# Splitting w2 in five staggered parts, and two key products on GpSimd

## The chip, the cores and the metric

One Trainium2 chip, one of its cores. The metric is the device time of one launch in microseconds (us). The engines of the core are TensorE (PE: matmul; PEld: weight load), VectorE (DVE), ScalarE (ACT), GpSimd (POOL) and SyncE (SP, which here only issues DMAs). Each engine runs its own instructions in the order in which the program gives them; an instruction that waits for a semaphore holds up all that stand behind it on that engine.

## What is computed

Polynomial sketch attention, whose result is the input of four dense experts that are mixed by normalized weights:

```python
def phi(x):
    a = np.einsum('rd,bhsd->bhsr', S1, x)
    b = np.einsum('rd,bhsd->bhsr', S2, x)
    return np.einsum('bhsi,bhsj->bhsij', a, b).reshape(*x.shape[:-1], r * r)
q_p, k_p = (phi(q), phi(k))
kv = np.einsum('bhsf,bhsd->bhfd', k_p, v)
z = np.sum(k_p, axis=2)
num = np.einsum('bhsf,bhfd->bhsd', q_p, kv)
den = np.einsum('bhsf,bhf->bhs', q_p, z)[..., None] + 1e-06
...
x = np.ascontiguousarray(attn_out.transpose(0, 2, 1, 3)).reshape(B * S, H * D)
p = domain_probs / (domain_probs.sum(-1, keepdims=True) + 1e-09)
for e in range(E):
    h = np.maximum(x @ w1[e], 0.0)
    out += p[:, e:e + 1] * (h @ w2[e])
```

The sizes: 4 batches, 4 heads, 1088 positions, head size 32, sketch size r = 8; 4352 tokens of width 128, 4 experts, hidden size 1024. All is float32.

## The kernel before

**Products of three matmuls.** A full float32 matmul of 448 columns stands in the profile as two matmuls of 0.92 us together (L1256), one of the `float32r` kind as one of 0.37 us. Most of the experts' matmuls are therefore made of three `float32r` ones, for which weights and data are split into a rounded part and rests:

- Tokens: `token_parts(m)` makes `xa` (ScalarE, `split`), `xb` and `xd` (VectorE, `join`) of one chunk of tokens.
- w1: `weight_part` makes `wa` (ScalarE), `wb` and `wd` (VectorE) of half an expert's w1. The list `SPLITS` has the step behind which each of these stands.
- w2: `second_weight_parts(e)` is a generator that makes `vab`, `vb` and `vd` of six of the eight row blocks of an expert's w2 (768 columns, handled as 256 and 512). It first splits with scale 4096 (ScalarE) and takes the difference (`join` on VectorE: the low part), then splits again with scale 1 over the same place (ScalarE), then forms `vd` (VectorE). The list `W2_AT` gives, for experts 2, 3, 0 and 1 in this order, the half step at which each next part of the generator is issued.

`split` is line 900 and `join` line 903 of the profile, whatever they are applied to. `vab` of an expert has the tag of that expert's w1, so it stands in the memory that held w1: its first split must wait until `wa` and `wb` have been made of it. The second split writes over what the low part was computed from, so it waits for VectorE's `join`.

**Steps and half steps.** The tokens go in 11 chunks m (`CHUNKS`: 128, 448, 480, 480, six of 448, 128). A step i is one chunk, one expert and one pair of hidden blocks (16 steps for each chunk), and has two half steps j; half step number 2i + j. In a half step of the chunks 1 to 9, `first` issues on TensorE `xa` by `wa` (L1150) and `xb` by `wb` (L1151) into a PSUM tile h; on ScalarE a correction of that tile in place (L1152); then, by `third`, for the half step before, `xd` by `wd` on top of it (L1202), and on ScalarE the rounded relu of it (`ha`, L1206, or the whole `hid`, L1211). `lower` issues the rests `hb` (L1178) and, for each pair, `hd` (L1181) on VectorE. So L1202 of one half step waits for L1152 of the same tile, and whatever ScalarE has ahead of that L1152 can hold up TensorE.

Then `work()` runs, and issues what the lists give for this half step: first the parts of w2 (`at_half`, from `W2_AT`, counted from 0), and then the entries of `plan` (counted from 1, so that entry 48 of `plan` comes in the same half step as entry 47 of `W2_AT`). What stands in `to_part` (the parts of w1 by `SPLITS`, the tokens by step 16m - 4 and 16m - 3) comes behind both half steps of a step.

**Products with w2.** `behind` issues what is due on TensorE. In chunk 1, experts 0 and 1 are taken `whole` (L1256, float32, `second`); from expert 2 on six blocks go in three matmuls (`passed`, L1275), in an order and at due times given by `DEAL` (a name such as a0 is the part and the block, the number its due half step, counted from the first of that expert). Two PSUM tiles, o0 and o1, hold the sums; `gather` adds them on VectorE (`ev`, L1304 and L1307) and multiplies with the gate and sums up on GpSimd (L1314, L1316).

**Attention beside it.** The attention of the later batches runs in between, by `plan`. `key_pieces(b, ...)` lays out the keys of batch b by `KEYS_AT[b]`: three transposes of k (L413), three projections on TensorE (L457) that ScalarE copies (L460), three sums (`fs`, L467), and then the four `key_product`s (L473, 128 x 576 elements each, all on VectorE) that make the factors `kp`; `key_sums` needs them only at entry 79. `UNITS_AT` lays out queries: products (L800), and a visit (`unit_visit`, `unit_project`, L683 to L709) with small matmuls at entry 47.

What matters for the change, for batch 1:

```python
    W2_AT = (36, 37, 38, 39), (40, 41, 42, 43), (44, 45, 46, 46), (50, 51, 53, 54)
    ...
        1: ((36, 37, 38), (38, 39, 40), (39, 40, 41), (51, 54, 60, 66)),
```

Of the kernel before, what the change touches and what calls it, by code (L numbers as in the profile page):

```python
# [17 lines left out]
def _ap(t, p0: int, np_: int, off: int, free):  # L18

    p = list(t.ap)[0]  # L20
    return bass.AP(t.tensor, t.offset + p0 * p[0] + off, [[p[0], np_]] + [list(d) for d in free])
# [3 lines left out]
def kernel(  # L25
# [24 lines left out]
    nc = tc.nc  # L50
# [9 lines left out]
    NT = 9  # L60
# [30 lines left out]
    ]  # L91
    W2_AT = (36, 37, 38, 39), (40, 41, 42, 43), (44, 45, 46, 46), (50, 51, 53, 54)
    TOKENS_AT = 11, 12

    CHUNKS = [P, 448, 480, 480] + [448] * 6 + [P]
# [15 lines left out]
    def psum(pool, tag):  # L111
        return pool.tile([P, 512], F32, tag=tag, name=tag)
# [32 lines left out]
    def load_batch(b):  # L145
        load_rows(k, b, "kn")
        vn[b] = load_v(b)
# [129 lines left out]
    low = _ap(s_raw, 0, R2, 0, [[2, D]])  # L277
# [133 lines left out]
    def key_turn(b, r, t0=0, n=4):  # L411
        if r < 2:
            nc.vector.transpose(  # L413
                _ap(kT, 0, P, 512 * r + P * t0, [[P, n], [32, 4], [1, 32]]),
                _ap(kn[b], 0, P, P * r + 32 * t0, [[32, n], [8 * D, 4], [1, 32]]),
            )
        else:
            nc.vector.transpose(kT[:, 1024:S], kn[b][:, 1024:S])

    def value_copy(b):  # L420
        copy = nc.gpsimd.tensor_copy if b == 1 else nc.scalar.copy
        for r in range(2):
            copy(
                vx[:, 4 * r : 4 * r + 4, :, 0:D].rearrange("p t h d -> p h t d"),
                _ap(vn[b], 0, P, P * r, [[8 * D, H], [D, 4], [1, D]]),
            )
            yield
        copy(vx[0:64, 8, :, 0:D], _ap(vn[b], 0, 64, 1024, [[D, H], [1, D]]))
# [21 lines left out]
    def key_project_wide(b, gi, kf):  # L450

        t0, n = FG[gi]
        if gi == 0:
            fss[b] = apool.tile([P, 2, NT, 32], F32, tag="fs", name="fs")
            kps[b] = apool.tile([P, NT, 2, P], F32, tag="kp", name="kp")
        for t in range(n):
            nc.tensor.matmul(  # L457
                kf[:, P * t : P * t + P], kT[:, P * (t0 + t) : P * (t0 + t + 1)], sk[:, :], start=True, stop=True
            )
        nc.scalar.copy(  # L460
            _ap(fss[b], 0, P, 32 * t0, [[32 * NT, 2], [32, n], [1, 32]]), _ap(kf, 0, P, 0, [[32, 2], [P, n], [1, 32]])
        )

    def key_add(b, gi, kf):
        t0, n = FG[gi]
        fs = _ap(fss[b], 0, P, 32 * t0, [[32 * NT, 2], [32, n], [1, 32]])
        nc.vector.tensor_tensor(out=fs, in0=_ap(kf, 0, P, HP, [[32, 2], [P, n], [1, 32]]), in1=fs, op=ALU.add)  # L467

    def key_product(b, t0, n, p, x, eng, kf=None):

        if b:
            fs = lambda k, dims: _ap(fss[b], 0, P, 32 * (NT * p + t0) + R2 * x + k, [[32, n]] + dims)
            eng.tensor_tensor(  # L473
                out=_ap(kps[b], 0, P, 256 * t0 + P * p + R * x, [[256, n], [R2, R], [1, R]]),
                in0=fs(0, [[1, R], [0, R]]), in1=fs(R, [[0, R], [1, R]]), op=ALU.mult,
            )
            return
        src, off = (kf, P * p) if kf is not None else (fss[b], 32 * (NT * p + t0))
        eng.tensor_tensor(
            out=_ap(kps[b], 0, P, 256 * t0 + P * p + 64 * x, [[256, n], [32, 2], [R, 4], [1, R]]),  # L480
            in0=_ap(src, 0, P, off + 4 * x, [[32, n], [R2, 2], [1, 4], [0, R]]),
            in1=_ap(fss[b], 0, P, 32 * (NT * p + t0) + R, [[32, n], [R2, 2], [0, 4], [1, R]]),
            op=ALU.mult,
        )
# [35 lines left out]
    def key_pieces(b, turn, project, summed, products):  # L520

        for r in range(3):
            add(turn[r], lambda r=r: key_turn(b, r))
        values, kf = value_copy(b), {}

        def project_keys(gi):
            kf[gi] = psum(ps_h, "h")
            key_project_wide(b, gi, kf[gi])

        def sum_keys(gi):  # L530
            key_add(b, gi, kf[gi])
            next(values, None)
            if gi == 2 and 1 < b < B - 1:
                load_batch(b + 1)

        for gi in range(3):
            add(project[gi], lambda gi=gi: project_keys(gi))
            add(summed[gi], lambda gi=gi: sum_keys(gi))
        for i, (p, x) in enumerate(((0, 0), (0, 1), (1, 0), (1, 1))):
            add(products[i], lambda p=p, x=x: key_product(b, 0, NT, p, x, nc.vector))  # L540

    sums = {}

# [205 lines left out]
    turned, factors, products = {}, {}, {}  # L749
# [59 lines left out]
    def add(hs, run):  # L809

        plan.setdefault(hs, []).append(run)

    FIRST_AT = (1, 2, 4, 5, 7, 9, 10, 12, 14, 15, 15, 15, 17, 18, 18, 19, 21, 23, 23)
    KEYS_AT = {
# [3 lines left out]
    }  # L818
# [6 lines left out]
    def lay_plan():  # L825
# [31 lines left out]
        for b in range(1, B):  # L857
            key_pieces(b, *KEYS_AT[b])
            if b > 1:
                add(UNITS_AT[{2: 2, 3: 4}[b]][3], lambda b=b: key_end(b))  # L860
# [38 lines left out]
    def split(a, w, scale):  # L899
        nc.scalar.activation(a, w, ACTF.Copy, scale=scale * NEAR)  # L900

    def join(out, in0, scale, in1, op):
        nc.vector.scalar_tensor_tensor(out=out, in0=in0, scalar=scale, in1=in1, op0=ALU.mult, op1=op)  # L903

    def weight_part(what, e, h):

        c = slice(F // 2 * h, F // 2 * (h + 1))
        w, a, b, d = (x[:, c] for x in (w1_of[e], wa[:, e], wb[:, e], wd[:, e]))
        if what == "a":
            split(a, w, 4096.0)  # L910
        elif what == "b":
            join(b, w, -4096.0, a.bitcast(F32), ALU.add)
        else:
            join(d, a.bitcast(F32), -R12, b.bitcast(F32), ALU.subtract)
# [3 lines left out]
    def second_weight_parts(e):  # L918


        w, n = w2_of[e, 0], N3 * DM
        vab = cpool.tile([P, F], F32R, tag=f"w1_{e}", name="vab")
        vb = cpool.tile([P, 2 * n - F], F32R, tag=f"vb_{e}", name="vb")
        a, lows = vab[:, 0:n], [(0, F - n, vab[:, n:F]), (F - n, n, vb[:, :])]
        for c, z, b in lows:
            split(a[:, c:z], w[:, c:z], 4096.0)
            join(b, w[:, c:z], 4096.0, a[:, c:z].bitcast(F32), ALU.subtract)
            yield
        for c, z, b in lows:
            split(a[:, c:z], w[:, c:z], 1.0)  # L930
            if c == 0:
                yield
        d = cpool.tile([P, n], F32R, tag=f"w2_{e}0", name="vd")[:, :]
        for c, z, b in lows:
            join(d[:, c:z], b.bitcast(F32), 1.0, a[:, c:z].bitcast(F32), ALU.subtract)
        w2_parts[e] = {
            THREE[i]: tuple(
                x[:, DM * i - c : DM * i - c + DM] for x, c in ((a, 0), next((x, c) for c, z, x in lows if DM * i < z), (d, 0))
            )
            for i in range(N3)  # L940
        }
        yield
# [393 lines left out]
    def at_step(step, *calls):  # L1336
        to_part.setdefault(step, []).extend(calls)
# [4 lines left out]
    for what, e, h, step in SPLITS:  # L1342
        at_step(step, lambda p=(what, e, h): weight_part(*p))
    for e, at in zip((2, 3, 0, 1), W2_AT):
        parts_of = second_weight_parts(e)
        for hs in at:
            at_half.setdefault(hs, []).append(next_of(parts_of))
# [135 lines left out]
```

## Time and profile before

| | |
|---|---|
| median of 3 runs | 447.97 us (447.76 to 448.28) |
| the profiled execution, its own time | 448.23 us |
| its span in the profile | 446.5 us |
| TensorE busy | 440.3 us, 2988 matmuls |
| TensorE weight loads | 370.7 us |
| VectorE busy | 380.5 us, 627 instructions |
| ScalarE busy | 335.0 us, 715 instructions |
| GpSimd busy | 135.5 us, 219 instructions |
| granted TensorE clock | 1.00 |

How to read it: in the timeline a row has the start in us, the length in us, the engine, the line of the kernel, the operation, the tile written and the tiles read, the shapes and the number of instructions; in brackets the idle time of the engine just before, and what ended it. In the table of stretches a row has the stretch, its length, the busy time of each engine with the number of instructions, then the granted clock, the share of the DMA engines and GB/s. A row of the waits has who waited for whom, the sum in us, how often, and the longest. Lengths of neighbouring instructions overlap a little, since they are pipelined; the distance of two starts is what one costs its engine.

### The profile page before, as it was taken

How to read it: one execution, taken by the hardware profiler on the slowest of the kernel's cores; microseconds unless marked ns; L12 is line 12 of the kernel's file. 1: busy time of each engine (PE TensorE's matmuls, PEld its weight loads, DVE VectorE, ACT ScalarE, POOL GpSimd, SP SyncE). 2: the span in 40 equal slices, each digit the busy share in tenths (PEclk: the TensorE clock that was granted, in tenths of full speed). 3: DMA queues.
4: the chain of work that ended last, by engine and by line, in shares of the span. 5: the costliest groups of instructions: out<-in, count | busy, mean ns of one | idle time of the engine just before them, and what ended most of it. 6: DMA issues, size and time to landing. Idle time of an engine off the chain costs nothing.

```text
span 446.5 us, 8575 instructions
## 1 busy us (share of the span) xinstructions
PE 440.3 (99%) x2988; PEld 370.7 (83%) x2988; DVE 380.5 (85%) x627; ACT 335.0 (75%) x715; POOL 135.5 (30%) x219
## 2 busy tenths in 40 slices
PE   9999899999999999999999999999999999999997
PEld 6887568878887888888888888888888888888886
DVE  5997879988999889888987888899988898898853
ACT  4477888867877588868875888787888888888831
POOL 7348324210143123213321333133323413331430
PEclk9999999999999999999999999999999999999999
DMA  6966257323702250145014601351300020027401
GB/s 186 282 176 169 62 132 156 94 45 96 186 22 46 67 145 22 49 92 153 22 39 69 146 21 27 77 139 46 66 21 21 24 61 22 21 38 221 156 2 28
DMA packets 51155, 38.46 MB, mean 86 GB/s; under 512 B 24968, under 2 KB 45384, under 8 KB 51112
## 3 DMA queue, kind: packets, MB, share of 16 engines
q1 hardware_dynamic: 49672, 36.79, 32.4%
q0 software_dynamic: 1216, 1.06, 1.0%
q8 instruction: 23, 0.38, 0.4%
q14 instruction: 20, 0.16, 0.1%
q10 hardware_dynamic: 224, 0.07, 0.1%
HBM read 32.68 MB, written 5.21 MB: 85 GB/s over the span
## 4 chain that ended last, share of the span: by engine, by line
PE 96%; DVE 2%; DMA 1%; ACT 1%; issue 1%; SPq 0%
PE o L1275 40%; PE h L1202 13%; PE h L1150 13%; PE h L1151 13%; PE h L262 9%; PE o L262 3%; PE o L1256 2%; PE h L457 1%; DMA kn<-in_k_dram 1%; DVE wb L903 0%; ACT h L1152 0%; PE h L1120 0%; DVE kp L473 0%; DVE vd L903 0%; DVE hb L1178 0%
## 5 line engine op out<-in xcount | busy, mean ns | idle before, releaser
L1152 ACT ACTIVATE h<-h 128x448 f32<-128x448 f32 (+1 forms) x288 | 155.4, 540 | 69.2 <-PE h L1151 63.2
L1178 DVE SCALAR_TENSOR_TENSOR hb<-h,ha 128x448 fp32r<-128x448 f32 (+1 forms) x219 | 133.9, 623 | 28.6 <-ACT ha L1206 25.7
L1181 DVE SCALAR_TENSOR_TENSOR hd<-ha,hb 128x896 fp32r<-128x896 f32 (+3 forms) x117 | 130.3, 1114 | 10.9 <-PE o L1275 0.9
L1150 PE MATMUL h<-xa,wa 128*128 128x448 f32 (+1 forms) x288 | 129.4, 449 | 0.0
L1206 ACT ACTIVATE ha<-h 128x448 fp32r<-128x448 f32 (+1 forms) x219 | 120.1, 549 | 0.0
L1314 POOL TENSOR_TENSOR ev<-ev,gate 128x256 f32<-128x256 f32 (+2 forms) x54 | 49.5, 917 | 216.2 <-DVE ev L1307 203.9
L1202 PE MATMUL h<-xd,wd 128*128 128x448 f32 (+1 forms) x288 | 107.2, 372 | 1.2 <-ACT h L1152 1.2
L1151 PE MATMUL h<-xb,wb 128*128 128x448 f32 (+1 forms) x288 | 106.2, 369 | 0.0
L1275 PE MATMUL o<-ha,vab 128*128 128x448 f32 (+1 forms) x204 | 75.7, 371 | 0.0
L1150 PEld LDWEIGHTS h<-xa,wa 128*128 128x128 f32 x288 | 54.2, 188 | 16.8 <-issue 12.1
L1151 PEld LDWEIGHTS h<-xb,wb 128*128 128x128 f32 x288 | 54.2, 188 | 16.7 <-issue 12.4
L1202 PEld LDWEIGHTS h<-xd,wd 128*128 128x128 f32 x288 | 54.0, 188 | 10.1 <-ACT h L1152 3.7
L1275 PE MATMUL o<-hd,vd 128*128 128x448 f32 (+1 forms) x204 | 61.6, 372 | 0.0
L1275 PE MATMUL o<-hb,vb 128*128 128x448 f32 (+1 forms) x136 | 50.1, 368 | 0.0
L1275 PE MATMUL o<-hid,w_sb 128*128 128x448 f32 (+1 forms) x106 | 49.3, 547 | 0.4 <-DVE ev L1304 0.4
L1316 POOL TENSOR_TENSOR total<-total,ev 128x256 f32<-128x256 f32 (+2 forms) x54 | 45.8, 848 | 4.2
L1275 PEld LDWEIGHTS o<-hd,vd 128*128 128x128 f32 x204 | 37.8, 188 | 4.5 <-issue 0.8
L1275 PEld LDWEIGHTS o<-ha,vab 128*128 128x128 f32 x204 | 38.3, 188 | 3.7
L1211 ACT ACTIVATE hid<-h 128x448 f32<-128x448 f32 (+1 forms) x69 | 38.1, 552 | 1.0 <-PE h L1202 0.8
L1314 POOL TENSOR_TENSOR total<-ev,gate 128x256 f32<-128x256 f32 (+2 forms) x18 | 12.3, 706 | 60.8 <-issue 41.5
L1275 PEld LDWEIGHTS o<-hb,vb 128*128 128x128 f32 x136 | 25.6, 188 | 2.3
L1275 PE MATMUL o<-hb,vab 128*128 128x448 f32 (+1 forms) x68 | 25.0, 368 | 0.0
(156 smaller groups left out, 462.7 us busy)
## 6 DMA issues: line engine op xcount, KB each, us to landing
gate<-gates SPq DMA_DIRECT2D x22, 224.0 KB, 3.3
kn<-in_k_dram SPq DMA_DIRECT2D x4, 544.0 KB, 6.7
vn<-in_v_dram SPq DMA_DIRECT2D x16, 128.0 KB, 5.1
qp<-qd SPq DMA_DIRECT2D x8, 256.0 KB, 3.3
w_last<-in_moe_w_dram SPq DMA_DIRECT2D x4, 512.0 KB, 4.9
qp<-qd SPq DMA_DIRECT2D x6, 288.0 KB, 4.9
qb<-qd SPq DMA_DIRECT2D x6, 288.0 KB
w_sb<-in_moe_w_dram SPq DMA_DIRECT2D x3, 512.0 KB
```

The source lines that it names most:

```text
L262: nc.tensor.matmul(out(s), weights(s), moving(s), **flags)
L1150: nc.tensor.matmul(g, wa[:, e, w], xa, start=True, stop=False)
L1151: nc.tensor.matmul(g, wb[:, e, w], xb, start=False, stop=True)
L1152: nc.scalar.activation(g, g, ACTF.Copy, scale=1.0 + R12)
L1178: nc.vector.scalar_tensor_tensor(out=hb, in0=g, scalar=0.0, in1=high, op0=ALU.max, op1=ALU.subtract)
L1181: nc.vector.scalar_tensor_tensor(out=d2, in0=a2.bitcast(F32), scalar=R12, in1=b2.bitcast(F32), op0=ALU.mult, op1=ALU.subtract)
L1202: nc.tensor.matmul(g, w, x, start=False, stop=True, skip_group_check=True)
L1206: nc.scalar.activation(ha, g, ACTF.Relu, scale=NEAR)
L1211: nc.scalar.activation(hid[i][j], g, ACTF.Relu)
L1275: nc.tensor.matmul(acc[m, e][o][:, 0:n], w, h, start=first_one, stop=last)
L1314: nc.gpsimd.tensor_tensor(out=to[:, x], in0=ev[:, x], in1=g[:, x], op=ALU.mult)
L1316: nc.gpsimd.tensor_tensor(out=total[m][:, x], in0=total[m][:, x], in1=ev[:, x], op=ALU.add)
```

## The change

1. `second_weight_parts` gives five parts in place of four, and VectorE's work lags ScalarE's by one part. Before: (split 256, low 256), (split 512, low 512), (second split 256), (second split 512, both `vd`). After: (split 256), (split 512, low 256), (second split 256, low 512), (second split 512), (both `vd`).
2. `W2_AT` has five half steps for each expert. Expert 2's are 36 to 40, expert 3's 40 to 44, expert 0's 45, 46, 47, 47, 49, and expert 1's are spread over 54, 57, 60, 63, 66.
3. Of the four key products of batch 1 the first and third go to GpSimd, and the entries are 48, 48, 52, 65 in place of 51, 54, 60, 66. The other batches keep VectorE and their entries.

The instructions and their sizes are otherwise the same; the order on TensorE and the order of DMAs on SP's and GpSimd's queues do not change.

```diff
-    W2_AT = (36, 37, 38, 39), (40, 41, 42, 43), (44, 45, 46, 46), (50, 51, 53, 54)
+    W2_AT = (36, 37, 38, 39, 40), (40, 41, 42, 43, 44), (45, 46, 47, 47, 49), (54, 57, 60, 63, 66)
...
-            add(products[i], lambda p=p, x=x: key_product(b, 0, NT, p, x, nc.vector))
+            eng = nc.gpsimd if b == 1 and i % 2 == 0 else nc.vector
+            add(products[i], lambda p=p, x=x, eng=eng: key_product(b, 0, NT, p, x, eng))
...
-        1: ((36, 37, 38), (38, 39, 40), (39, 40, 41), (51, 54, 60, 66)),
+        1: ((36, 37, 38), (38, 39, 40), (39, 40, 41), (48, 48, 52, 65)),
...
-        for c, z, b in lows:
-            split(a[:, c:z], w[:, c:z], 4096.0)
+        first_part, other_part = (slice(c, z) for c, z, _ in lows)
+
+        def low(c, z, b):
             join(b, w[:, c:z], 4096.0, a[:, c:z].bitcast(F32), ALU.subtract)
-            yield
-        for c, z, b in lows:
-            split(a[:, c:z], w[:, c:z], 1.0)
-            if c == 0:
-                yield
+
+        split(a[:, first_part], w[:, first_part], 4096.0)
+        yield
+        split(a[:, other_part], w[:, other_part], 4096.0)
+        low(*lows[0])
+        yield
+        split(a[:, first_part], w[:, first_part], 1.0)
+        low(*lows[1])
+        yield
+        split(a[:, other_part], w[:, other_part], 1.0)
+        yield
```

## The prediction, made before the changed kernel was run

> **What bounds the kernel now.** I read the page's engine shares first, then the waits of TensorE, then stretches of time, and last the order of instructions around each wait.
>
> ```profile
> PE 440.3 (99%) x2988; PEld 370.7 (83%) x2988; DVE 380.5 (85%) x627; ACT 335.0 (75%) x715; POOL 135.5 (30%) x219
> ...
> PE h L1202 <- ACT h L1152: 1.2, 1, 1.2
> ...
> PE o L1275 <- DVE ev L1304: 0.4, 1, 0.4
> ...
> 40.00:50.00 10.00, 8.78 (x34) 5.80 (x33) 7.43 (x15) 7.47 (x18) 5.69 (x10) 1.00 0.51 134
> 60.00:70.00 10.00, 9.58 (x43) 7.56 (x42) 9.63 (x15) 8.53 (x20) 3.87 (x4) 1.00 0.75 174
> 76.00:84.00 8.00, 8.00 (x38) 6.85 (x37) 7.76 (x12) 7.09 (x15) 2.63 (x3) 1.00 0.13 37
> 200.00:430.00 230.00, 229.99 (x1235) 200.09 (x1233) 202.00 (x299) 184.37 (x388) 66.61 (x78) 1.00 0.27 68
> ```
>
> TensorE is busy for 440.3 of 446.5 us, at a granted clock of 1.00. Only the stretches 40 to 50 us (8.78 busy of 10) and 60 to 70 us (9.58) show holes that an order of the other engines can close; from 200 to 430 us nothing is left (229.99 of 230). So the change can gain about two microseconds at most, or lose by opening new holes. TensorE's own order is the same before and after; what moves is the order on ScalarE, VectorE and GpSimd. With TensorE full behind the changed stretch, a hole closed or opened there reaches the end one for one.
>
> **The first hole, at 44.6 us.** Rows of the timeline, one engine after the other:
>
> ```profile
> 42.05 0.43 DVE L903 SCALAR_TENSOR_TENSOR vd<-vab 128x256 fp32r<-128x256 f32 x1 [2.21 <-ACT vab L900]
> ...
> 42.99 0.42 DVE L467 TENSOR_TENSOR fs<-h,fs 128x256 f32<-128x256 f32 x1
> 43.33 1.75 DVE L903 SCALAR_TENSOR_TENSOR wb<-w_sb,wa 128x512 fp32r<-128x512 f32 x2
> ...
> 41.38 0.63 ACT L900 ACTIVATE vab<-w_sb 128x512 fp32r<-128x512 f32 x1
> ...
> 45.11 0.42 ACT L900 ACTIVATE vab<-w_sb 128x256 fp32r<-128x256 f32 x1 [1.97 <-DVE wb L903]
> 45.43 0.53 ACT L1152 ACTIVATE h<-h 128x448 f32<-128x448 f32 x1
> ...
> 43.06 0.37 PE L1151 MATMUL h<-xb,wb 128*128 128x448 f32 x1
> 43.26 0.37 PE L1202 MATMUL h<-xd,wd 128*128 128x448 f32 x1
> ...
> 44.43 0.37 PE L1151 MATMUL h<-xb,wb 128*128 128x448 f32 x1
> 46.01 0.47 PE L1202 MATMUL h<-xd,wd 128*128 128x448 f32 x1 [1.22 <-ACT h L1152]
> ```
>
> VectorE sits 2.21 us at `vd` of expert 2 until ScalarE's last split (41.38) is done, and the two `wb` of expert 3 stand behind that. The first split of expert 3's w2 overwrites the buffer that `wb` reads (`vab` has the tag of that w1), so ScalarE sits 1.97 us, and behind it stands the correction L1152 for which TensorE waits. Two matmuls of this width start 0.20 us apart (43.06, 43.26), so L1202 was due at 44.63 and came at 46.01: 1.38 us lost.
>
> In the changed order `vd` is a part of its own, in half step 40; the two `wb`, emitted after step 19 (half steps 38 and 39), stand before it, behind a second `fs` that waits for a ScalarE copy issued ahead of the 41.38 split. VectorE is free at 42.05 - 2.21 = 39.84; `fs` (42.99 to 43.33: 0.34) and both `wb` (1.75) end near 41.9. ScalarE asks for that buffer at 45.11 - 1.97 = 43.14. The wait goes with 1.2 us to spare: **-1.38**. Next late there would be ScalarE's own queue, with two activations and a split in each half step; behind 46.01 the trace shows it keeping pace with that load, since the stretch 40 to 50 lacks 10 - 8.78 = 1.22 us, which is this one wait.
>
> **The second hole, at 63.6 us.**
>
> ```profile
> 60.20 0.62 DVE L1178 SCALAR_TENSOR_TENSOR hb<-h,ha 128x448 fp32r<-128x448 f32 x1 [0.67 <-ACT ha L1206]
> 60.85 1.09 DVE L1181 SCALAR_TENSOR_TENSOR hd<-ha,hb 128x896 fp32r<-128x896 f32 x1
> 61.86 0.42 DVE L903 SCALAR_TENSOR_TENSOR vab<-w_sb,vab 128x256 fp32r<-128x256 f32 x1
> 62.20 0.75 DVE L473 TENSOR_TENSOR kp<-fs 128x576 f32<-128x576 f32 x1
> 62.87 0.68 DVE L903 SCALAR_TENSOR_TENSOR vb<-w_sb,vab 128x512 fp32r<-128x512 f32 x1
> 63.47 0.62 DVE L1304 COPY ev<-o 128x448 f32<-128x448 f32 x1
> ...
> 63.35 0.37 PE L1275 MATMUL o<-ha,vab 128*128 128x448 f32 x1
> 64.14 1.02 PE L1275 MATMUL o<-hid,w_sb 128*128 128x448 f32 x2 [0.42 <-DVE ev L1304]
> ```
>
> The copy `ev` frees the accumulator that TensorE wants at 63.35 + 0.20 = 63.55, and stands behind three instructions of 1.61 us (61.86 to 63.47). All three leave this place: expert 1's splits begin at entry 54 and not 50, and the key product goes to an earlier half step. In their stead comes the `vd` pair of expert 0 ahead of the second `hb`; the pair takes 0.94 (42.05 to 42.99), of which 0.67 fills idle time. The copy then ends near 62.7, 0.8 us early: **-0.59**. What is next late is `vd` itself, which expert 0's first use in the next block of tokens does not need for some twenty half steps.
>
> **The third, small one.** A split of 512 columns on ScalarE (entry 54) makes the correction late once:
>
> ```profile
> 66.47 0.63 ACT L900 ACTIVATE vab<-w_sb 128x512 fp32r<-128x512 f32 x1
> ...
> 67.24 0.36 PE L1151 MATMUL h<-xb,wb 128*128 128x448 f32 x1
> 67.59 0.47 PE L1202 MATMUL h<-xd,wd 128*128 128x448 f32 x1
> ```
>
> The step is 0.35 instead of 0.20. At that entry now stands the 256 part (0.42 in place of 0.63 long): **-0.15**.
>
> **What it adds.** Three places put more on ScalarE just ahead of a correction.
>
> ```profile
> 53.05 1.14 PE L262 MATMUL h<-qT,sx 128*64 128x288 f32 x8
> ...
> 55.68 0.75 DVE L696 TENSOR_TENSOR xs<-h,rc 128x384 f32<-128x384 f32 x2
> 56.47 0.71 DVE L709 STREAM_TRANSPOSE y<-xs 128x512 f32<-128x512 f32 x1
> ...
> 56.45 0.55 ACT L1152 ACTIVATE h<-h 128x448 f32<-128x448 f32 x1
> ...
> 57.62 0.36 PE L1202 MATMUL h<-xd,wd 128*128 128x448 f32 x1
> ...
> 69.77 0.61 ACT L900 ACTIVATE xa<-ring 128x480 fp32r<-128x480 f32 x1
> 70.26 0.55 ACT L1152 ACTIVATE h<-h 128x448 f32<-128x448 f32 x1
> ...
> 70.95 0.38 PE L1202 MATMUL h<-xd,wd 128*128 128x448 f32 x1
> ```
>
> Half step 47 (`47, 47`) now holds two splits where it held none (before, the double split lay in 46, ahead of the small matmuls of a visit, which hid it). A 256 split holds ScalarE for 0.32 (45.11 to 45.43; it is 0.42 long, so neighbours overlap by 0.10), a 512 split for 0.63 - 0.10 = 0.53. The correction at 56.45 begins 0.85 later, at 57.30, ends at 57.85, and reaches TensorE 0.05 on (46.01 against 45.43 + 0.53), at 57.90. It is wanted at 57.62: **+0.28**. The second of these splits must also wait until `vb` has read what it overwrites, and `vb` stands on VectorE behind `xs` and `y`. Those wait for TensorE's matmul at 53.05, which ends at 54.19. In times of before: 54.2 + 0.05 + 0.75 + 0.71 + 0.68 gives 56.4 for the end of `vb`; ScalarE is there at 56.45 + 0.32 = 56.77. Cover: 0.4 us.
>
> Entry 57 puts a 512 split right ahead of the split `xa` of the next tokens (69.77, also after half step 57). The correction at 70.26 ends at 70.81 and reaches TensorE at 70.86, 0.09 before its 70.95; 0.53 more makes **+0.44**. Entry 63 holds the other 512 split, alone: bounds 0 and 0.44, nearest row the 0.15 at 67.59, which I take: **+0.15**. The 256 parts (54, 60) I take at 0, between 0 and 0.1 each; they are 0.2 shorter than the split that cost 0.15.
>
> VectorE gets `vb`, `vd` and one key product between 72 and 84 us in place of two key products: 0.60 + 0.94 - 0.67 = 0.87 more (62.87 to 63.47, the pair above, 62.20 to 62.87) where it is busy 7.76 of 8. The bounds are 0 and 0.87. I take 0: the slots in `DEAL` give its results several half steps, TensorE is 8.00 of 8 busy there now, and the stretch before lost 1.61. Expert 1's last part comes at half step 66 and its first matmul is due at 76.
>
> GpSimd takes two products. No row shows this form on it there; the nearest are:
>
> ```profile
> L1314 POOL TENSOR_TENSOR ev<-ev,gate 128x256 f32<-128x256 f32 (+2 forms) x54 | 49.5, 917 | 216.2 <-DVE ev L1307 203.9
> ...
> 7.71 1.21 POOL L479 TENSOR_TENSOR kp<-fs 128x256 f32<-128x256 f32 x2 [0.48 <-ACT fs L446]
> ...
> 50.08 1.85 POOL L1314 TENSOR_TENSOR total<-ev,gate 128x256 f32<-128x256 f32 x2 [3.79 <-DVE ev L1304]
> ...
> 50.24 1.22 DVE L903 SCALAR_TENSOR_TENSOR vd<-vb,vab 128x512 fp32r<-128x512 f32 x1
> ```
>
> By 1.21 us for 512 elements one product of 576 takes 1.4 us, by 917 ns for about 228 it takes 2.3: two end 2.7 to 4.6 us after `total` (51.93 in before), at 54.6 to 56.5 in times of before and earlier if `ev` moves up. Behind them on GpSimd stands the gating of the next expert, which waits for the `ev` copy (62.7 by the step above), so nobody is late. The change issues no DMA and moves none on SP's or GpSimd's queue. Beside `total`, a `vd` of VectorE took 1.22 where the `vb` row of the same shape has 0.68: 0.54 more that is GpSimd's doing. The products will do the same to what VectorE runs beside them; the bounds are 0 and four times 0.54, the cover is 0.4 before `vb` and the 0.67 of idle before 60.20, and I take 0 because VectorE loses its wait of 2.21 and, ahead of `xs`, the two `vd` of expert 0.
>
> **Sum.** -1.38 - 0.59 - 0.15 + 0.28 + 0.44 + 0.15 = -1.25 us. The profiled execution took 448.23 (span 446.5), so 446.98 by its own time; the median of three lies 0.26 below it, at 447.97: **446.7**.
>
> **Rivals.**
>
> *ScalarE pays it back.* If every split in the dense stage is exposed in full (0.32 + 0.53 + 0.32 + 0.53 of expert 1, 0.85 in half step 47), the cost is 2.55 against the 2.12 gained: 448.4. For it: one split of 512 already cost 0.15 there. Against: four splits of the same sizes stand in that stage before, and its 9.58 of 10 is explained by the wait of 0.42. Half of that cost gives 447.1. Chance 0.2.
>
> *GpSimd holds VectorE back (slower).* The place is `vb` before the double split. Each microsecond by which `vb` ends later than 0.4 us of cover stops ScalarE, with all corrections behind it. If VectorE's instructions with two operands in SBUF cannot run until both products are through, at 56.5 by the slow price, then `vd` of expert 3 begins there, and `xs`, `y` and `vb` follow: 56.5 + 0.94 + 0.75 + 0.71 + 0.68 = 59.6 against 56.8: +2.8, less the 1.25 gained, 449.5. It turns into a loss once `vb` ends 1.25 us after ScalarE's 56.8. The Trainium skill ("SBUF — State Buffer", Who interferes with whom) says just this: a GpSimd instruction and a VectorE one with two SBUF inputs exclude each other, and the first to start holds the shared ports to its end. By that rule the trace agrees in kind and not in size: 0.54 was lost beside 1.85 of GpSimd. Chance 0.1.
>
> *No new hole.* Removing the waits may shift ScalarE ahead of TensorE. If ScalarE absorbs the additions, only the 2.12 stand: 445.9. Chance 0.1.
>
> **Numbers.** The forecast has 0.6. This kernel can tell about 0.2%, 0.9 us, from no change: faster means below 447.07. The forecast (its own spread 446.2 to 447.0) and "no new hole" make faster 0.70; ScalarE's payback makes most of the same, 0.20; GpSimd's lock slower, 0.10. The range reaches from the 445.9 of the last rival, less 0.1, to 448.2, into the payback, and leaves out the lock and the payback's end.
>
> **What would show it.** Right: no wait of `L1152`'s successor over 0.5 us near 44 us; ScalarE's 1.97 and VectorE's 2.21 gone; no TensorE wait for `ev`; one new wait of 0.2 to 0.3 after the double split and one of 0.4 beside `xa`; GpSimd products of 1.4 to 2.3 us. Wrong: ScalarE idle before the second split of half step 47, waiting for `vb`; or TensorE waits at 76 to 84 us for VectorE's `hb` or `hd`.

## The result: 446.13 us, and the profile after

The changed kernel takes **446.13 us** (median of 6 runs, 445.99 to 446.42). The kernel before takes 448.13 beside it (6 runs, 447.76 to 448.28). The ratio is 0.9957, with a 95% interval of 0.9945 to 0.997: faster by 0.30 to 0.55%. The profiled execution took 446.1, with a span of 444.3 (2.1 and 2.2 less than the profiled execution of before). In the code after, lines are shifted: `split` is L901, `join` L904, L1151 to L1159, L1152 to L1160, L1202 to L1210, L1256 to L1264, L1275 to L1283, L1304 to L1312. The experiments have shifts of their own; there the tiles tell which row is meant.

From the page and from the waits of TensorE, after:

```profile
PE 438.4 (99%) x2988; PEld 370.2 (83%) x2988; DVE 380.1 (86%) x625; ACT 335.0 (75%) x715; POOL 138.3 (31%) x221
...
PE h L1210 <- ACT h L1160: 0.3, 1, 0.3
```

The wait of 1.2 us for the correction and the one of 0.4 for `ev` are gone; one new wait of 0.3 for a correction has come. (A wait of 1.2 for GpSimd's `sr`, which the kernel before does not show, ends at 6.10 us, far ahead of everything that was changed; the profiled executions differ there from one to the next.) The same stretches as before, and that from 70 to 84 us for a later comparison:

```profile
40.00:50.00 10.00, 10.00 (x40) 6.88 (x38) 9.73 (x17) 9.22 (x21) 8.14 (x13) 1.00 0.51 137
60.00:70.00 10.00, 9.73 (x45) 8.11 (x44) 8.15 (x12) 8.57 (x20) 2.63 (x4) 1.00 0.93 204
70.00:84.00 14.00, 14.00 (x62) 11.14 (x60) 13.00 (x20) 11.39 (x25) 4.79 (x6) 1.00 0.24 52
76.00:84.00 8.00, 8.00 (x36) 6.15 (x34) 7.21 (x12) 6.50 (x15) 0.78 (x3) 1.00 0.08 23
```

The stretch 40 to 50 is full (10.00, was 8.78). The one from 60 to 70 still lacks 0.27: the second hole is closed there, and another is opened.

The timeline of TensorE, after, at the places of the prediction, in order of time:

```profile
44.17 0.37 PE L1159 MATMUL h<-xb,wb 128*128 128x448 f32 x1
44.37 0.37 PE L1210 MATMUL h<-xd,wd 128*128 128x448 f32 x1
...
55.56 0.37 PE L1159 MATMUL h<-xb,wb 128*128 128x448 f32 x1
56.00 0.47 PE L1210 MATMUL h<-xd,wd 128*128 128x448 f32 x1
...
61.83 0.37 PE L1283 MATMUL o<-ha,vab 128*128 128x448 f32 x1
62.04 0.91 PE L1283 MATMUL o<-hid,w_sb 128*128 128x448 f32 x2
...
68.32 0.37 PE L1159 MATMUL h<-xb,wb 128*128 128x448 f32 x1
68.96 0.47 PE L1210 MATMUL h<-xd,wd 128*128 128x448 f32 x1 [0.27 <-ACT h L1160]
69.27 0.57 PE L1283 MATMUL o<-hd,vd 128*128 128x448 f32 x2
...
76.72 0.38 PE L1159 MATMUL h<-xb,wb 128*128 128x480 f32 x1
77.07 0.49 PE L1210 MATMUL h<-xd,wd 128*128 128x480 f32 x1
```

At 44.37 and at 62.04 the matmul starts 0.20 and 0.21 after the one ahead of it: both old holes are gone. At 56.00, 68.96 and 77.07 stand the three new ones, 0.44, 0.64 and 0.35 after the matmul ahead where 0.20 to 0.22 is due. Behind a hole the next matmul is late as well: 69.27 is 0.31 after 68.96.

VectorE, ScalarE and GpSimd at these places:

```profile
40.24 1.28 DVE L904 SCALAR_TENSOR_TENSOR wb<-w_sb,wa 128x512 fp32r<-128x512 f32 x2
42.70 0.42 ACT L901 ACTIVATE vab<-w_sb 128x256 fp32r<-128x256 f32 x1
43.43 1.42 POOL L423 COPY vx<-vn 128x512 f32<-128x512 f32 x2
...
53.74 0.65 DVE L904 SCALAR_TENSOR_TENSOR vb<-w_sb,vab 128x512 fp32r<-128x512 f32 x1
54.58 0.94 ACT L901 ACTIVATE vab<-w_sb 128x256 fp32r<-128x256 f32 x2
60.48 0.62 DVE L1312 COPY ev<-o 128x448 f32<-128x448 f32 x1
67.35 0.63 ACT L901 ACTIVATE vab<-w_sb 128x512 fp32r<-128x512 f32 x1
67.87 0.61 ACT L901 ACTIVATE xa<-ring 128x480 fp32r<-128x480 f32 x1
```

The two `wb` end at 41.52, 1.18 before ScalarE's split at 42.70, which now has no wait in brackets. The double split at 54.58 runs without a gap (0.94 for both), so it did not wait for `vb` (53.74 to 54.39).

### The profile page after: what moved, and what is told of

Read it like the earlier page. It is cut to its first block, busy times and chain, and to the rows that moved or that the text cites. A ratio compares the mean times of both kernels' runs of the same rounds, so it can differ in the third digit from the quotient of the medians.

```text
span 444.3 us, 8576 instructions
## 1 busy us (share of the span) xinstructions
PE 438.4 (99%) x2988; PEld 370.2 (83%) x2988; DVE 380.1 (86%) x625; ACT 335.0 (75%) x715; POOL 138.3 (31%) x221
## 4 chain that ended last, share of the span: by engine, by line
PE 93%; DVE 2%; ACT 2%; DMA 1%; issue 1%; SPq 0%; DVEq 0%; ACTq 0%
PE o L1283 39%; PE h L1210 13%; PE h L1158 13%; PE h L1159 13%; PE h L262 7%; PE o L1264 3%; PE o L262 3%; PE h L457 1%; DMA kn<-in_k_dram 1%; DVE qp L594 1%; ACT h L1160 0%; DMA vn<-in_v_dram 0%; ACT vab L901 0%; ACT ha L1214 0%; PE h L1128 0%
## 5 line engine op out<-in xcount | busy, mean ns | idle before, releaser
L1160 ACT ACTIVATE h<-h 128x448 f32<-128x448 f32 (+1 forms) x288 | 155.3, 539 | 68.4 <-PE h L1159 64.1
L1322 POOL TENSOR_TENSOR ev<-ev,gate 128x256 f32<-128x256 f32 (+2 forms) x54 | 48.6, 901 | 215.7 <-DVE ev L1315 207.2
L1210 PE MATMUL h<-xd,wd 128*128 128x448 f32 (+1 forms) x288 | 107.1, 372 | 0.4 <-ACT h L1160 0.3
L1159 PE MATMUL h<-xb,wb 128*128 128x448 f32 (+1 forms) x288 | 106.1, 368 | 0.0
L1283 PE MATMUL o<-ha,vab 128*128 128x448 f32 (+1 forms) x204 | 75.7, 371 | 0.0
L1159 PEld LDWEIGHTS h<-xb,wb 128*128 128x128 f32 x288 | 54.2, 188 | 16.7 <-issue 12.4
L1283 PE MATMUL o<-hd,vd 128*128 128x448 f32 (+1 forms) x204 | 61.6, 372 | 0.0
L1210 PEld LDWEIGHTS h<-xd,wd 128*128 128x128 f32 x288 | 54.0, 188 | 8.9 <-ACT h L1160 2.7
L1283 PE MATMUL o<-hb,vb 128*128 128x448 f32 (+1 forms) x136 | 50.1, 368 | 0.0
L1283 PE MATMUL o<-hid,w_sb 128*128 128x448 f32 (+1 forms) x106 | 49.3, 546 | 0.0
L1283 PEld LDWEIGHTS o<-hd,vd 128*128 128x128 f32 x204 | 37.9, 188 | 4.5 <-issue 0.8
L1283 PEld LDWEIGHTS o<-ha,vab 128*128 128x128 f32 x204 | 38.3, 188 | 3.8
L1283 PEld LDWEIGHTS o<-hb,vb 128*128 128x128 f32 x136 | 25.5, 188 | 2.3
L1283 PE MATMUL o<-hb,vab 128*128 128x448 f32 (+1 forms) x68 | 25.1, 368 | 0.0
```

The lines of the kernel that those rows point to most:

```text
L1159: nc.tensor.matmul(g, wb[:, e, w], xb, start=False, stop=True)
L1160: nc.scalar.activation(g, g, ACTF.Copy, scale=1.0 + R12)
L1210: nc.tensor.matmul(g, w, x, start=False, stop=True, skip_group_check=True)
L1283: nc.tensor.matmul(acc[m, e][o][:, 0:n], w, h, start=first_one, stop=last)
L1322: nc.gpsimd.tensor_tensor(out=to[:, x], in0=ev[:, x], in1=g[:, x], op=ALU.mult)
```

## The experiments

Two theories stood at the beginning. **A**, that of the prediction: the time follows from single places where ScalarE's or VectorE's order makes TensorE late, and GpSimd's two products are beside the point. **B**: the products on GpSimd matter, by relieving VectorE or by holding it up. In each diff below the lines with + are those of the experiment.

The experiments ran on two chips, on which the kernel before has medians of 448.05 and 448.24 us. Each ratio is against the runs of the kernel before beside it, and these scatter widely; kernels are therefore compared with each other by their medians.

**The first hole alone.** The kernel before, with the five-part order for experts 2 and 3 only:

```diff
-    W2_AT = (36, 37, 38, 39), (40, 41, 42, 43), (44, 45, 46, 46), (50, 51, 53, 54)
+    W2_AT = (36, 37, 38, 39, 40), (40, 41, 42, 43, 44), (44, 45, 46, 46), (50, 51, 53, 54)
...
+        if e > 1:
+            split(a[:, first_part], w[:, first_part], 4096.0)
+            ...
+        else:
+            for c, z, b in lows:
+                split(a[:, c:z], w[:, c:z], 4096.0)
+            ...
```

> The kernel before with the new order of splits for experts 2 and 3 alone; experts 0 and 1 and all four key products as before. Theory A (the gain is the first hole, and the scatter of the kernel before comes from it): the first hole is gone (-1.38 and -0.1 for the weight load behind it), the second stays with its 0.6 to 0.7; 446.4 to 446.7, and all runs within 0.6 us of each other. Theory B (the scatter and part of the gain have another source, such as the chip): runs still spread over 2 us, median 447.0 or more.

446.07 us (5 runs, 446.06 to 446.34), ratio 0.9939 (0.9917 to 0.9961): as fast as the whole change, and 0.33 below the range that was expected. All runs lie within 0.28. From its waits of TensorE:

```profile
PE o L1293 <- DVE ev L1322: 0.4, 1, 0.4
```

The wait for the correction is gone and the one for `ev` is still there. So the new order for experts 2 and 3 alone brings as much as the whole change, and everything else in the change comes out at about nothing. With the two traces lined up matmul by matmul, everything else takes away the second hole and the third (-0.70 and -0.21, with the late matmul behind each) and adds the three new ones (+0.34, +0.52, +0.21), +0.16 together; the medians differ by 0.06. The first hole itself is 1.48 of the 2.16 us between this trace and the first one of before; most of the rest lies at places that no term of the prediction names (see "What the sum missed").

**The splits alone.** The changed kernel with the products on VectorE at the entries of before:

```diff
-            eng = nc.gpsimd if b == 1 and i % 2 == 0 else nc.vector
+            eng = nc.vector
...
-        1: ((36, 37, 38), (38, 39, 40), (39, 40, 41), (48, 48, 52, 65)),
+        1: ((36, 37, 38), (38, 39, 40), (39, 40, 41), (51, 54, 60, 66)),
```

> Only the five-part splits and their half steps; all four key products on VectorE at the entries of before (51, 54, 60, 66). Theory A (three holes of TensorE close because of the order on VectorE and ScalarE): the hole at 46.0 us goes (1.41 and 0.10 of restart behind it), and the one at 64.1 too, since only one product of 0.67 us is left ahead of the ev copy, which then ends near 61.8 for a matmul due at 62.0. So the full gain: 2.0 us faster than before, no more than 0.2 from the changed kernel. Theory B (the gain beyond the first hole is VectorE's relief by GpSimd): 0.5 to 0.7 us slower than the changed kernel, that is 1.3 to 1.5 us faster than before.

446.91 us (12 runs, 446.64 to 447.62), ratio 0.9963 (0.9948 to 0.9978). Both old holes are gone, but it is 0.78 slower than the changed kernel, so theory A falls: the splits alone do not give the full gain. The 1.14 below the kernel before (448.05 beside it) are a little less than theory B had. The stretch 70 to 84 us of this kernel, and the rows of it that matter:

```profile
70.00:84.00 14.00, 13.89 (x59) 10.74 (x58) 13.70 (x19) 11.43 (x24) 4.26 (x5) 1.00 0.17 42
...
71.59 0.75 DVE L473 TENSOR_TENSOR kp<-fs 128x576 f32<-128x576 f32 x1
...
79.43 0.75 DVE L473 TENSOR_TENSOR kp<-fs 128x576 f32<-128x576 f32 x1
...
83.04 0.38 PE L1283 MATMUL o<-ha,vab 128*128 128x480 f32 x1
83.53 0.67 PE L1283 MATMUL o<-hid,w_sb 128*128 128x480 f32 x1
```

VectorE is busy 13.70 of 14 us there, with two products; in the changed kernel, with one, it is 13.00. Lined up with the changed kernel, TensorE loses 0.17 at 66.6 (another product, at 64.57, is ahead), 0.26 at 77.3 and 0.38 at 83.53 (0.49 behind its neighbour instead of 0.21), and wins 0.19 at 68.7: 0.62, of 0.78 between the medians. (The two profiled executions also differ by 0.2 to 0.3 ahead of 22 us, the other way, and by 0.20 at 346 us.) So the products do belong to the change: with expert 1's splits spread to half step 66, VectorE has too little room for products at entries 54 and 60 as well. Which of the two moved parts of the product edit does it, the engine or the entry, the next kernel tells.

**The products at the new entries, all on VectorE:**

```diff
-            eng = nc.gpsimd if b == 1 and i % 2 == 0 else nc.vector
+            eng = nc.vector
```

> The changed kernel, with all four key products left on VectorE at the new entries 48, 48, 52, 65. Theory A: VectorE idles 2.28 us before its first hb and takes the two products of 0.67 there and in the 0.8 us before 62.9: within 0.2 us of the changed kernel, and the vd, vd, vab beside GpSimd's products shrink from 0.95, 1.08 and 1.40 us to 0.42, 0.68 and 0.42. Theory B: 0.5 us or more slower than the changed kernel.

446.15 us (7 runs, 445.96 to 446.47), ratio 0.9945 (0.9925 to 0.9965): the changed kernel to 0.02 us. Theory B falls: it is the entry that counts, and GpSimd takes nothing off TensorE's path. What it does to VectorE is seen by setting the two traces beside each other. The changed kernel first, then three rows of this one:

```profile
50.22 1.40 DVE L904 SCALAR_TENSOR_TENSOR vab<-w_sb,vab 128x256 fp32r<-128x256 f32 x1
49.71 1.63 POOL L473 TENSOR_TENSOR kp<-fs 128x576 f32<-128x576 f32 x1
51.30 1.35 POOL L473 TENSOR_TENSOR kp<-fs 128x576 f32<-128x576 f32 x1
```

```profile
48.90 0.94 DVE L904 SCALAR_TENSOR_TENSOR vd<-vab 128x256 fp32r<-128x256 f32 x1
49.77 1.08 DVE L904 SCALAR_TENSOR_TENSOR vd<-vb,vab 128x512 fp32r<-128x512 f32 x1
50.77 0.41 DVE L904 SCALAR_TENSOR_TENSOR vab<-w_sb,vab 128x256 fp32r<-128x256 f32 x1
```

The same `vab` takes 0.41 on its own and 1.40 beside the first product. It ends at 51.62, 0.28 after that product (51.34), while the second product goes on to 52.65. So it waited for one GpSimd instruction, not for both, and lost 0.99 us in 2.94 of GpSimd. The two `vd` were expected to shrink as well and did not: they take 0.94 and 1.08 with no product beside them, as in the changed kernel (0.95 and 1.08). GpSimd's `total` runs beside them in both (here from 48.46 to 50.30), so they are not the products' doing.

**Four products on GpSimd:**

```diff
-            eng = nc.gpsimd if b == 1 and i % 2 == 0 else nc.vector
+            eng = nc.gpsimd if b == 1 else nc.vector
```

> The changed kernel with all four key products of the second batch on GpSimd instead of two, at the same entries. Theory A (GpSimd only stretches what VectorE runs beside it, and the cover is enough): three products in a row take about 4.4 us on GpSimd instead of 2.9, VectorE loses about 1 us more but two products of 0.7 leave it; vb ahead of the double split is not later; 445.9 to 446.4. Theory B (the lock): VectorE loses what GpSimd runs, 1.5 us more, vb comes later than its 0.4 us of cover and ScalarE waits before the second split of half step 47; 446.8 to 448.

446.75 us (7 runs, 446.43 to 447.37), ratio 0.9953 (0.9935 to 0.9971), between the two expectations. From its timeline:

```profile
49.42 4.07 POOL L473 TENSOR_TENSOR kp<-fs 128x576 f32<-128x576 f32 x3
53.38 0.67 DVE L904 SCALAR_TENSOR_TENSOR vb<-w_sb,vab 128x512 fp32r<-128x512 f32 x1
54.22 0.94 ACT L901 ACTIVATE vab<-w_sb 128x256 fp32r<-128x256 f32 x2
```

Three products in a row take 4.07 us, and yet `vb` is not late and the double split runs through: the place that the rival named does not give way under a third more GpSimd work. No new hole shows from 30 to 230 us; behind that, far from the products, stand two steps of 0.26 and 0.31 us that the changed kernel does not have, at 234 and 301 us. The profiled execution is also the fastest of the seven, and where the others lose 0.1 to 0.9 us more it does not show. Why this kernel is 0.62 slower than the changed one stays open.

**Other places for the splits of experts 0 and 1.** Each new hole comes from a split that falls on a half step with something else in it, so this kernel moves those three:

```diff
-    W2_AT = (36, 37, 38, 39, 40), (40, 41, 42, 43, 44), (45, 46, 47, 47, 49), (54, 57, 60, 63, 66)
+    W2_AT = (36, 37, 38, 39, 40), (40, 41, 42, 43, 44), (44, 45, 46, 47, 49), (50, 52, 54, 61, 66)
```

> The changed kernel with other half steps for experts 0 and 1: 44, 45, 46, 47, 49 (no double split in 47) and 50, 52, 54, 61, 66 (splits where ScalarE idles 0.4 to 0.5 us; none beside the tokens' xa). Theory A: the new holes at 56.0 (0.26 and 0.11 of restart), 69.0 (0.43 and 0.09) and 77.1 (0.11 and 0.10) go: 0.9 to 1.1 us faster than the changed kernel, near 445.1 us. Theory B: no change against the changed kernel, since VectorE's load stays the same.

**445.23 us** (6 runs, 444.97 to 445.58), ratio 0.9923 (0.99 to 0.9945): 0.90 below the changed kernel, and the fastest of all. One of its stretches, and a row of VectorE:

```profile
60.00:70.00 10.00, 10.00 (x47) 8.37 (x47) 9.38 (x14) 9.18 (x20) 2.81 (x4) 1.00 0.91 211
...
51.88 1.66 DVE L904 SCALAR_TENSOR_TENSOR vb<-w_sb,vab 128x512 fp32r<-128x512 f32 x1
```

From 60 to 70 us TensorE is now busy 10.00 of 10. Lined up with the changed kernel, the three places with the matmul behind each are 0.30, 0.53 and 0.24 shorter. The forecast's +0.28, +0.44 and +0.15 were real costs, and all three could be avoided. In this kernel both products on GpSimd hit VectorE: `vab` takes 1.40, and `vb` behind it 1.66 in place of 0.65. TensorE does not wait for either.

**The products alone.** The kernel before, with the products as in the change:

```diff
-            add(products[i], lambda p=p, x=x: key_product(b, 0, NT, p, x, nc.vector))
+            eng = nc.gpsimd if b == 1 and i % 2 == 0 else nc.vector
+            add(products[i], lambda p=p, x=x, eng=eng: key_product(b, 0, NT, p, x, eng))
...
-        1: ((36, 37, 38), (38, 39, 40), (39, 40, 41), (51, 54, 60, 66)),
+        1: ((36, 37, 38), (38, 39, 40), (39, 40, 41), (48, 48, 52, 65)),
```

> Only the key products: two on GpSimd, entries 48, 48, 52, 65; the splits in four parts as before. Theory A: the first hole stays at 1.4 us; ahead of the ev copy are left the two parts of the split, 0.94 in place of 1.61 us, so the copy ends 0.67 earlier and the second hole shrinks from 0.59 to about 0.1: 0.5 to 0.7 us faster than before. Theory B: 1 us or more faster than before, because VectorE is freed in the whole stage. If GpSimd's port time decides (rival of the prediction): slower than before.

448.70 us (12 runs, 447.34 to 450.57), ratio 1.0001 (0.9981 to 1.0021): inconclusive for the time, since the runs lie over three microseconds. So do those of the kernel before: 41 runs on two chips, from 447.48 to 450.37. None of the kernels without the first hole does this (widest range: 0.98 us). In the profiled execution of this kernel, 449.57 us, the second hole shrinks by 0.7, and the first is larger. Its waits, stretches and matmuls of TensorE:

```profile
PE h L1203 <- ACT h L1153: 2.1, 1, 2.1
...
40.00:50.00 10.00, 7.95 (x28) 5.20 (x27) 7.54 (x14) 6.64 (x17) 6.01 (x11) 0.88 0.53 141
48.00:51.00 3.00, 3.00 (x7) 2.00 (x6) 3.00 (x6) 2.39 (x6) 0.15 (x1) 0.50 0.14 35
...
48.40 0.57 PE L1152 MATMUL h<-xb,wb 128*128 128x448 f32 x1
48.77 0.57 PE L1203 MATMUL h<-xd,wd 128*128 128x448 f32 x1
```

TensorE waited 2.1 us instead of 1.2, and behind it the granted clock falls: it is 0.50 from 48 to 51 us, with matmuls 0.37 apart where 0.20 is usual. Lined up with the kernel before, that slow piece costs 1.55 us on top of the longer wait. Why the wait was longer is seen in VectorE's second `wb` beside GpSimd's copies of the second batch's values. From this kernel, then from the kernel before:

```profile
43.85 1.99 DVE L904 SCALAR_TENSOR_TENSOR wb<-w_sb,wa 128x512 fp32r<-128x512 f32 x1
44.11 0.63 POOL L423 COPY vx<-vn 128x512 f32<-128x512 f32 x1
44.67 0.63 POOL L423 COPY vx<-vn 128x512 f32<-128x512 f32 x1
```

```profile
43.92 1.15 DVE L903 SCALAR_TENSOR_TENSOR wb<-w_sb,wa 128x512 fp32r<-128x512 f32 x1
43.89 0.63 POOL L423 COPY vx<-vn 128x512 f32<-128x512 f32 x1
44.45 1.11 POOL L423 COPY vx<-vn 128x512 f32<-128x512 f32 x1
```

With two copies in its span the `wb` takes 1.99, with one ahead of it 1.15. In the second case the next copy is the one that is held up (1.11 instead of 0.63). The starts alone do not tell who gets in first: the `wb` of 1.99 starts 0.26 ahead of the first copy, and yet ends 0.54 behind the second (45.84, 45.30). When the copies start depends on a DMA: GpSimd's instruction ahead of them waits for `qb` to land, and they begin at 43.89 in the kernel before, at 44.11 here and at 44.46 in the second trace below.

**The kernel before, once more, for a second trace:**

> The kernel before once more, for a second trace. Theory A: between its two traces the first hole differs by the length of the two wb (1.75 in the first), or the small steps of 0.17 at 139 us and 0.22 at 244 us are absent; the second hole is 0.59 in both. Theory B (the holes are fixed): both traces agree within 0.1 us at every hole.

447.94 us. The waits of TensorE, and VectorE and GpSimd at the same place:

```profile
PE h L1202 <- ACT h L1152: 0.8, 1, 0.8
PE h L262 <- DVE qp L800: 0.4, 1, 0.4
PE o L1275 <- DVE ev L1304: 0.4, 1, 0.4
...
43.60 0.68 DVE L903 SCALAR_TENSOR_TENSOR wb<-w_sb,wa 128x512 fp32r<-128x512 f32 x1
44.46 0.63 POOL L423 COPY vx<-vn 128x512 f32<-128x512 f32 x1
```

Here the first copy comes 0.18 after the second `wb` is done, so this `wb` takes 0.68 and the first hole is 0.49 shorter. A `vab` is hit by the copies instead (1.16), and 0.50 comes back in a wait for `qp` behind it. So theory A holds for the first hole. The second hole is the same, and the small steps at 139 and 244 us are as in the first trace.

**Without the copies.** The kernel before; the copies of the second batch's values are left out, and that batch reads the first batch's:

```diff
+        if b == 1:
+            yield
+            yield
+            return
         copy = nc.gpsimd.tensor_copy if b == 1 else nc.scalar.copy
```

> The kernel before, without GpSimd's copies of the second batch's values (the batch reads the first batch's values instead). Theory A (these copies lengthen the two wb of expert 3 by a varying amount, that lengthens the first hole, and a hole over some 2 us is followed by a lower granted clock): the two wb take 1.3 us instead of 1.75 to 2.59, the first hole shrinks from 1.38 to about 0.9, no run is over 448.0, median 447.0 to 447.4. Theory B (the length of the hole or the clock varies for another reason): runs near 448.8 and 450.2 stay, the median is within 0.3 of the kernel before.

447.52 us (10 runs, 447.35 to 447.83), ratio 0.9978 (0.9963 to 0.9992). The median lies 0.1 over the 447.0 to 447.4 that was expected; the rest came as expected, from its timeline:

```profile
43.03 1.28 DVE L907 SCALAR_TENSOR_TENSOR wb<-w_sb,wa 128x512 fp32r<-128x512 f32 x2
44.35 0.42 ACT L904 ACTIVATE vab<-w_sb 128x256 fp32r<-128x256 f32 x1 [1.51 <-DVE wb L907]
```

Both `wb` take 1.28, ScalarE waits 1.51, the first hole is 0.52 shorter than in the first trace of before, and the spread is gone (0.48 from end to end). That these copies make the scatter of the kernel before is shown; that the slowest runs (granted clock 0.995 to 0.996, 7 of the 41, 450.06 to 450.37) are those in which the wait passes some two microseconds was seen in one trace only, that of the kernel with the products alone. It is not the whole story: the slowest run of that kernel, 450.57, has a granted clock of 1.00.

## Why the prediction was right

It forecast 446.7 and the time is 446.13: the side and the range are right. The gain is 2.00 us by the medians (448.13 to 446.13) where 1.25 was forecast, so 0.75 was missed. Its steps beside what the starts of the 2988 matmuls show in the two profiled executions; the second number is the next matmul, which starts late behind each hole. The two executions differ by 2.13 in all:

| place (before) | forecast | trace |
|---|---|---|
| first hole, 46.01 | -1.38 | -1.41, -0.10 |
| second hole, 64.14 | -0.59 | -0.59, -0.11 |
| third, 67.59 | -0.15 | -0.15, -0.06 |
| double split, 57.62 | +0.28 | +0.26, +0.11 |
| 512 split beside `xa`, 70.95 | +0.44 | +0.43, +0.09 |
| entry 63, 78.86 | +0.15 | +0.11, +0.10 |
| visit, 52.53 | 0 | -0.14 |
| ahead of 30 us | 0 | -0.23 |
| behind 80 us (steps at 139 and 244) | 0 | -0.39 |
| sum | -1.25 | -2.08 |

**The six terms.** All lie within 0.04. Five of them were worked out at the place itself, from distances of starts, or from a length less the overlap of neighbours, and not from the bare lengths that the rows show. The sixth, entry 63, was taken over from the nearest row, between bounds of 0 and 0.44; that it came so close is in part luck. What the prediction put at 0 held too: no start moves by more than 0.05 at the 256 parts of expert 1, or between 80 and 138 us. The late matmul behind every hole was overlooked, but three holes went and three came, so it cancels (-0.27 and +0.30).

**What the sum missed** is 0.83 us, and 0.62 of it lies outside the changed stretch. The 0.23 at the start is not the change's: the second trace of the kernel before is 0.30 earlier there, too. The steps at 139 and 244 us stand in both traces of before and in that without the copies. They are gone in every kernel that has any part of the change, in the one with the products alone as in the one with the first hole alone, so neither the splits nor the products are needed for it. These two and the kernel with the splits alone have a new step of 0.20 instead, near 346 to 349 us. The runs do not settle the cause. The 0.14 at the visit stands at matmuls that wait for VectorE's `qp` (the wait of 0.4 in the second trace of before is at this place); it was not tested.

**A reading that was wrong, and cost nothing.** The 1.75 us of the two `wb` were taken as their length. Their own length is 1.28; the rest was GpSimd's copies, and changes from run to run. The hole that the change takes out was thus not 1.38 but something from 0.9 to 2.2, in the three traces that have the old order and the copies (1.38, 0.92 and 2.22); the changed kernel has both `wb` done 1.9 us ahead of the first copy (41.52, 43.43), and no such scatter. The forecast took one trace for the kernel, and that this was a typical one is luck: it took 448.23, and the 41 runs beside the experiments, from 447.48 to 450.37, have their median at 448.19.

**The rivals.** *ScalarE pays it back*: it did in the places named, and no more; the new holes take 1.10 with the late matmuls, a little more than the 0.91 that the second and third hole give, as the kernel with the first hole alone bears out. *GpSimd holds VectorE back*: the products took 1.63 and 1.35 us (forecast 1.4 to 2.3, so one is just under it), and the first did stop a `vab`. The Trainium skill ("SBUF — State Buffer", Who interferes with whom) has the two engines exclude each other for a whole instruction. The prediction held that the trace agrees in kind and not in size; taken instruction by instruction it agrees in size as well for this `vab`: 0.41 became 1.40, ending 0.28 after the product. What the rival had wrong was the lock's reach: VectorE came through between the two products, and the cover ahead of `vb` was never used up. That is no rule either: beside the shorter copies a `wb` (1.99) and a `vab` (1.16) came through only behind the second one. *No new hole*: three came. The kernel with other places is what this rival had forecast, 445.9, and does better, at 445.23.

## What to carry to other kernels

Where one engine is busy 99% of the span, line up its instructions in two traces and price each edit at the one place where it makes that engine late, by distances of starts on the engine that feeds it; that gave six terms to 0.04 us here. Then ask of each part of a change whether it pays alone: here one reordering, two `wb` ahead of a `vd`, brought as much as the whole change, and moving the rest away from half steps that were already loaded was worth 0.9 us more. If a kernel's runs scatter, look for two engines whose instructions meet by chance on the path, and order them apart.

## What the runs showed of the chip

- VectorE instructions with two operands in SBUF were held up beside GpSimd's: `wb` of 128 x 512 took 0.68, 1.15 or 1.99 us with none, one or two copies in its way, and `vab` of 128 x 256 took 0.41 or 1.40 without and with a product. GpSimd was held up in turn (a copy of 0.63 took 1.11). VectorE came through behind one GpSimd instruction in some cases and behind two in others; the runs do not show what decides it.
- After an idle time of 2.1 us TensorE ran matmuls 0.37 apart instead of 0.20, at a granted clock of 0.50 from 48 to 51 us, and lost 1.55 us. After 1.2 and 0.8 us idle the clock stayed at 1.00. The Trainium skill ("TensorE: Matmul & The Clock Gate", Part 1: The HAM clock gate) has the clock halved after an idle window of about 3.4 us whose start is not tied to the kernel. In pace the trace agrees (0.37 against 0.20); in the length of the idle time it does not, since 2.1 us were enough in the one trace that has such a wait.
- Behind each hole the next matmul was late as well, by 0.06 to 0.11 us: behind the first hole it started 0.31 after the one that had waited, not 0.20.
